# A fused short convolution and two-matrix SiLU block on one core: from 96-row chunks and PE transposes to two streams in 64-row halves of the array, in a pinned order

## The chip, the cores and the metric

The kernel runs on one core of a Trainium2 chip. The metric is the device time of one execution in microseconds (us), on an otherwise idle chip. Engines are named as the profile names them: PE is the matrix engine (PEld its weight loads), DVE the vector engine, ACT the activation engine, POOL and SP the two engines that here mostly issue DMAs. PSUM is the memory that PE writes its products to; "bank" stands here for one of the two parts, `[:, 0]` and `[:, 1]`, of a product tile in it; an eviction is the instruction that reads them out of it.

## The reference, cut to what matters

```python
# x: (8, 4096, 192)   weight: (8 heads, 7 taps)   w_in: (192, 2048)   w_out: (2048, 192)   beta: (2048,)
w   = softmax(weight, axis=-1)                      # one set of 7 taps for each group of 24 columns
c   = causal_conv7(x, w)                            # along the 4096 tokens; zeros before each batch's first token
h   = c.reshape(32768, 192) @ w_in
g   = h * sigmoid(beta * h)                         # = SiLU(beta * h) / beta
out = g @ w_out                                     # (32768, 192), float32
```

There are 32768 tokens. The first product contracts 192 columns, which does not split evenly into 128 rows, the most that a matmul in these traces has (L205 of the kernel before). The second contracts 2048.

## The kernel before

Tokens go through in 64 tiles of 512. Each tile is loaded (with a cast to bf16), transposed on PE, copied out of PSUM by DVE, convolved by DVE with columns on partitions, multiplied by `w_in` in two chunks of 96 rows, put through SiLU by ACT, and multiplied by `w_out`. `beta` is multiplied into `w_in` and divided out of `w_out` during start-up.

```python
for st in range(N_ST):                              # 64 tiles of 512 tokens
    nc.gpsimd.dma_start(out=x_bf, in_=x_view[st])
    ...                                             # L137/L138: 8 PE transposes into ptr, L142/L143: DVE copies
    for cw, xt, ct, rows in ((cw_a, xt_a, ct_a, DA), (cw_b, xt_b, ct_b, DB)):   # DA = DB = 96
        nc.vector.tensor_scalar_mul(ct[:rows, :], xt[:rows, 0:ST_TOK], cw[:rows, 0:1])
        for k in range(1, K - 1):
            nc.vector.scalar_tensor_tensor(out=ct[:rows, :], in0=xt[:rows, k:k + ST_TOK], ...)     # L163
        nc.vector.tensor_tensor(ct[:rows, :], xt[:rows, K - 1:K - 1 + ST_TOK], ct[:rows, :], ALU.add)  # L171
    for pair in range(NF // 2):                     # first product: NF = 16 chunks of 128 outputs
        ph = psum_h.tile([128, 2, ST_TOK], FP32)
        for i in range(2):
            fc = 2 * pair + i
            nc.tensor.matmul(ph[:, i, :], w_in_sa[:DA, ts(fc, 128)], ct_a[:DA, :], start=True, stop=False)  # L183
            nc.tensor.matmul(ph[:, i, :], w_in_sb[:DB, ts(fc, 128)], ct_b[:DB, :], start=False, stop=True)  # L190
        nc.scalar.activation(g_t[:, 2 * pair:2 * pair + 2, :], ph, AF.Silu)                        # L197
    for half in range(N_BLK // 2):                  # second product: 4 blocks of 128 tokens
        po = psum_o.tile([128, 2, D], FP32)
        for j in range(2):
            for fc in range(NF):
                nc.tensor.matmul(po[:, j, :], g_t[:, fc, ts(2 * half + j, BLK)], w_out_s[:, fc, :], ...)   # L205
        nc.vector.tensor_copy(o_sb[:, 2 * half:2 * half + 2, :], po)
    nc.sync.dma_start(out=out_view[st], in_=o_sb)
```

Nothing in it fixes the order in which an engine's work is issued; the framework's scheduler chooses it.

## Time and profile before

| | before |
|---|---|
| time, median of 4 runs | 1061.03 us |
| PE busy | 902.9 us, 85% |
| DVE, ACT busy | 60%, 48% |
| mean granted PE clock | 0.932 |
| PE waiting for the convolution | 114 us in 16 waits |

First the busy line of the page, its PE and PE-clock rows (40 equal slices, tenths), and three groups of instructions of the kernel before. A group's columns are: line, engine, operation, output and inputs, shapes, count | busy us, mean ns of one | idle time of the engine just before them, and what ended most of it.

```profile
PE 902.9 (85%) x6656; PEld 581.1 (55%) x6656; DVE 635.5 (60%) x1313; ACT 503.7 (48%) x516; POOL 49.1 (5%) x70
...
PE   1699798897979979799797988979799797997968
...
PEclk9999899898998989899898998989989899998989
...
L197 ACT ACTIVATE g_t<-ph 128x1024 bf16<-128x1024 f32 x512 | 500.5, 1021 | 540.8 <-PE ph L190 539.6
L183 PE MATMUL ph<-ct_a,w_in_sa 96*128 96x512 bf16 x1024 | 411.9, 402 | 118.7 <-DVE ct_a L171 114.3
...
L205 PE MATMUL po<-w_out_s,g_t 128*128 128x192 bf16 x4096 | 386.9, 247 | 2.7
```

The mean of 402 ns is the time from a matmul's start to its end, and matmuls overlap. What counts is the distance between starts. It is read in the timeline of PE (start us, length us, what; in brackets the idle time before and who ended it). Here is a stretch with a stall:

```profile
311.35 0.22 PE L138 MATMUL ptr<-ident,x_bf 128*96 128x128 bf16 x1
318.34 0.58 PE L183 MATMUL ph<-ct_a,w_in_sa 96*128 96x512 bf16 x1 [6.77 <-DVE ct_a L171]
318.73 0.63 PE L190 MATMUL ph<-ct_b,w_in_sb 96*128 96x512 bf16 x1
319.15 0.63 PE L183 MATMUL ph<-ct_a,w_in_sa 96*128 96x512 bf16 x1
...
325.25 0.38 PE L183 MATMUL ph<-ct_a,w_in_sa 96*128 96x512 bf16 x1
325.47 0.38 PE L190 MATMUL ph<-ct_b,w_in_sb 96*128 96x512 bf16 x1
```

The wait for the convolution over the whole run is one line of the list of waits (who waited for whom: us in total, times, longest):

```profile
PE ph L183 <- DVE ct_a L171: 114.3, 16, 11.4
```

In the stretch above, PE stands for 6.77 us until DVE has finished a convolution, then starts a 512-column matmul only every 0.425 us, and is back at 0.215 us some seven microseconds later. These are half and full clock: the view of windows gives a granted clock of 0.51 from 318.3 to 325.0 us and of 1.00 from 325.25 to 330.0 us. The clock record in the packed trace has the same after each of the 15 waits for the convolution that follow start-up (14 of 6.77 us, one of 8.12): a stretch at 0.50 that begins within the wait and lasts until 3.5 to 6.9 us after it.

### The profile page before, as it was taken

To read this page: it belongs to the slowest core of one execution; us is meant where nothing else is said; L and a number is where in the kernel's file an instruction comes from. 1 tells how busy PE (TensorE), PEld (TensorE's weight loads), DVE (VectorE), ACT (ScalarE), POOL (GpSimd) and SP (SyncE) were. 2 spreads that over 40 slices of the span, in tenths; PEclk is the share of its full clock that TensorE was granted. 3 is DMA by queue.
4 is the path that set the end of the run, shared out by engine and by line. 5 is a ranking of instruction groups with operands and counts; after the bars stand their busy time and mean duration, and the time that the engine had idled before them with its cause. 6 is when DMAs were issued, how large, how long until landed. Compare 5 with 4: busy or idle time off the path is not lost.

```text
span 1059.0 us, 15609 instructions
## 1 busy us (share of the span) xinstructions
PE 902.9 (85%) x6656; PEld 581.1 (55%) x6656; DVE 635.5 (60%) x1313; ACT 503.7 (48%) x516; POOL 49.1 (5%) x70
## 2 busy tenths in 40 slices
PE   1699798897979979799797988979799797997968
PEld 1366466464655646466464664646556464664645
DVE  5874564847547485464946548475474854649461
ACT  1355364453535535355353644535355352553534
POOL 2000000000000000000000000000000000000000
PEclk9999899898998989899898998989989899998989
DMA  9111312112130121301212121121201213012100
GB/s 208 12 38 38 53 32 42 32 38 38 38 54 15 38 39 38 53 16 38 41 45 44 32 43 31 38 38 38 53 16 38 38 38 53 16 38 39 37 16 31
DMA packets 72438, 42.96 MB, mean 41 GB/s; under 512 B 37232, under 2 KB 72048, under 8 KB 72048
## 3 DMA queue, kind: packets, MB, share of 16 engines
q0 software_dynamic: 33792, 12.59, 10.9%
q1 hardware_dynamic: 38576, 29.38, 8.7%
q8 instruction: 52, 0.85, 0.3%
q14 instruction: 18, 0.15, 0.0%
HBM read 29.37 MB, written 25.17 MB: 52 GB/s over the span
## 4 chain that ended last, share of the span: by engine, by line
PE 78%; DVE 13%; ACT 4%; DMA 2%; issue 1%; SPq 0%; ACTq 0%
PE po L205 33%; PE ph L183 24%; PE ph L190 21%; DVE ct_b L163 5%; DVE ct_a L163 5%; ACT g_t L197 4%; DMA beta_t<-in_moe_beta_dram 2%; DVE o_sb L212 1%; DVE ct_a L171 1%; DVE xt_b L143 1%; DVE xt_a L142 0%; DVE ct_b L159 0%; DVE ct_a L159 0%; DVE w_out_s L123 0%; SPq L78 0%
## 5 line engine op out<-in xcount | busy, mean ns | idle before, releaser
L197 ACT ACTIVATE g_t<-ph 128x1024 bf16<-128x1024 f32 x512 | 500.5, 1021 | 540.8 <-PE ph L190 539.6
L183 PE MATMUL ph<-ct_a,w_in_sa 96*128 96x512 bf16 x1024 | 411.9, 402 | 118.7 <-DVE ct_a L171 114.3
L190 PE MATMUL ph<-ct_b,w_in_sb 96*128 96x512 bf16 x1024 | 411.0, 402 | 0.0
L205 PE MATMUL po<-w_out_s,g_t 128*128 128x192 bf16 x4096 | 386.9, 247 | 2.7
L205 PEld LDWEIGHTS <-g_t 128*128 128x128 bf16 x4096 | 343.1, 98 | 71.0 <-ACT g_t L197 17.1
L212 DVE COPY o_sb<-po 128x384 f32<-128x384 f32 x128 | 71.1, 556 | 381.2 <-PE po L205 381.2
L163 DVE SCALAR_TENSOR_TENSOR ct_b<-xt_b,cw_b,ct_b 96x512 bf16<-96x512 bf16 x320 | 236.7, 740 | 0.0
L163 DVE SCALAR_TENSOR_TENSOR ct_a<-xt_a,cw_a,ct_a 96x512 bf16<-96x512 bf16 x320 | 236.6, 739 | 0.0
L190 PEld LDWEIGHTS <-w_in_sb 96*128 96x128 bf16 x1024 | 103.6, 101 | 233.2 <-issue 158.5
L183 PEld LDWEIGHTS <-w_in_sa 96*128 96x128 bf16 x1024 | 103.5, 101 | 125.8 <-issue 34.1
L133 POOL DMA_DIRECT2D x_bf<-in_x_dram x64 | 48.5, 760 | 905.1 <-PE ptr L138 903.9
L137 PE MATMUL ptr<-ident,x_bf 128*96 128x128 bf16 x256 | 39.1, 226 | 30.5 <-DMA x_bf<-in_x_dram 15.6
L137 PEld LDWEIGHTS <-x_bf 128*96 128x96 bf16 x256 | 31.0, 127 | 39.1 <-issue 17.5
L142 DVE COPY xt_a<-ptr 96x512 bf16<-96x512 bf16 x64 | 26.5, 413 | 22.4 <-PE ptr L138 22.4
L138 PE MATMUL ptr<-ident,x_bf 128*96 128x128 bf16 x256 | 38.6, 224 | 0.0
L138 PEld LDWEIGHTS <-x_bf 128*96 128x96 bf16 x256 | 31.0, 128 | 4.4
L171 DVE TENSOR_TENSOR ct_b<-xt_b,ct_b 96x512 bf16<-96x512 bf16 x64 | 26.5, 413 | 0.0
L171 DVE TENSOR_TENSOR ct_a<-xt_a,ct_a 96x512 bf16<-96x512 bf16 x64 | 26.4, 412 | 0.0
L143 DVE COPY xt_b<-ptr 96x512 bf16<-96x512 bf16 x64 | 26.2, 410 | 0.0
L159 DVE TENSOR_SCALAR ct_a<-xt_a,cw_a 96x512 bf16<-96x512 bf16 x64 | 23.0, 360 | 0.0
L159 DVE TENSOR_SCALAR ct_b<-xt_b,cw_b 96x512 bf16<-96x512 bf16 x64 | 21.8, 340 | 0.0
L150 DVE COPY xt_b<-xt_b 96x6 bf16<-96x6 bf16 x56 | 9.0, 160 | 0.0
(30 smaller groups left out, 25.8 us busy)
## 6 DMA issues: line engine op xcount, KB each, us to landing
out_dram<-o_sb SPq DMA_DIRECT2D x64, 384.0 KB
x_bf<-in_x_dram POOLq DMA_DIRECT2D x64, 192.0 KB, 5.2
w_out_t<-in_moe_w_out_dram SPq DMA_DIRECT2D x1, 1536.0 KB
beta_bc<-in_moe_beta_dram SPq DMA_DIRECT2D x1, 1024.0 KB
w_in_a<-in_moe_w_in_dram SPq DMA_DIRECT2D x1, 768.0 KB
w_in_b<-in_moe_w_in_dram SPq DMA_DIRECT2D x1, 768.0 KB
cw_a<-in_weight_dram SPq DMA_DIRECT2D x4, 0.7 KB
cw_b<-in_weight_dram SPq DMA_DIRECT2D x4, 0.7 KB
```

The lines of the kernel that those rows point to most:

```text
L133: nc.gpsimd.dma_start(out=x_bf, in_=x_view[st])
L137: nc.tensor.transpose(ptr[:DA, blk, :], x_bf[:, blk, 0:DA], ident)
L138: nc.tensor.transpose(ptr[:DB, N_BLK + blk, :], x_bf[:, blk, DA:D], ident)
L143: nc.vector.tensor_copy(xt_b[:DB, PAD:], ptr[:DB, N_BLK : 2 * N_BLK, :])
L159: nc.vector.tensor_scalar_mul(ct[:rows, :], xt[:rows, 0:ST_TOK], cw[:rows, 0:1])
L163: nc.vector.scalar_tensor_tensor(out=ct[:rows, :], in0=xt[:rows, k : k + ST_TOK], scalar=cw[:rows, k : k + 1], in1=ct[:rows, :], op0=mybir ...
L171: nc.vector.tensor_tensor(ct[:rows, :], xt[:rows, K - 1 : K - 1 + ST_TOK], ct[:rows, :], mybir.AluOpType.add,)
L183: nc.tensor.matmul(ph[:, i, :], w_in_sa[:DA, ts(fc, 128)], ct_a[:DA, :], start=True, stop=False,)
L190: nc.tensor.matmul(ph[:, i, :], w_in_sb[:DB, ts(fc, 128)], ct_b[:DB, :], start=False, stop=True,)
L197: nc.scalar.activation(g_t[:, 2 * pair : 2 * pair + 2, :], ph, AF.Silu)
L205: nc.tensor.matmul(po[:, j, :], g_t[:, fc, ts(blk, BLK)], w_out_s[:, fc, :], start=(fc == 0), stop=(fc == NF - 1),)
L212: nc.vector.tensor_copy(o_sb[:, 2 * half : 2 * half + 2, :], po)
```

## The change

The intent is to fill the array in the first product and to take everything else off PE.

- **Two streams in two halves.** The tokens are split into two streams of 16384. Columns of stream 0 live on partitions 0 to 63, those of stream 1 on 64 to 127; 192 columns are three chunks of 64. `w_in` is held on both halves. A matmul of stream 0 uses rows 0 to 63 of the array and one of stream 1 rows 64 to 127, so that the two can run together, if the array allows it.
- **The second product in halves too.** So that the array keeps one row tiling through the steady steps, each 128-row contraction is two 64-row ones, one in each half. The kernel keeps the halves from writing one PSUM bank at a time: they start on different banks and swap banks later ("phase").
- **A pinned order, one step ahead.** A unit is one `fc` of the first product of step i, a sixteenth of the second product of step i-1, and two DVE operations of the convolution of step i+1.
- **DMA transposes** in place of PE transposes, and **beta** as the activation's scale.
- **Start-up**: the first 128 tokens of each stream are convolved on PE by matmuls with shifted identities, and the first steps are short (128, 128, 256 tokens).

The core of the diff; start-up, launch and much of the bookkeeping are cut:

```diff
-        ptr = psum_tr.tile([128, 2 * N_BLK, BLK], BF16)
-        for blk in range(N_BLK):
-            nc.tensor.transpose(ptr[:DA, blk, :], x_bf[:, blk, 0:DA], ident)
-            nc.tensor.transpose(ptr[:DB, N_BLK + blk, :], x_bf[:, blk, DA:D], ident)
...
+            pin(nc.sync.dma_start_transpose(
+                out=xt_of[j][:, :, c:c + 128],
+                in_=xbf_of[j][:, b, :, :, :].rearrange("p k s c -> p (k s c)")))
...
+    def mm1(i, fc):
+        n = steps[i][1]
+        ph = psum_h.tile([128, NS, TILE], FP32, name="ph")
+        for kk in range(NK):                                     # NK = 3 chunks of 64
+            for s in range(NS):                                  # NS = 2 streams
+                r = slice(64 * s, 64 * s + 64)
+                pin(nc.tensor.matmul(ph[:, s, 0:n], w_in_s[r, kk, ts(fc, 128)], xc_of[i][r, kk, 0:n],
+                                     start=(kk == 0), stop=(kk == NK - 1)))
+        pin(nc.scalar.activation(g_of[i][:, fc, :, 0:n], ph[:, :, 0:n], AF.Silu,
+                                 scale=beta[:, fc:fc + 1]))
...
+    def mm2(i, pr, phase, fc):
...
+        for half in range(2):
+            q = half ^ phase                                     # bank of this half in this phase
+            s, b = pr[q]
+            r = slice(64 * half, 64 * half + 64)
+            pin(nc.tensor.matmul(po[:, q, 0:D], g_of[i][r, fc, s, ts(b, 128)], w_out_s[r, fc, :],
+                                 start=(phase == 0 and fc == 0), stop=(phase == 1 and fc == NF - 1)))
...
+        for u in range(NF):
+            mm1(i, u)
+            for t in plan[u]:                                    # 8 calls of mm2, in full steps
+                mm2(i - 1, *t)
+            for op in conv[:2]:                                  # convolution of step i + 1
+                op()
+            conv = conv[2:]
```

## The prediction

> **What bounds it now.** TensorE, by its own work and by a stall. In the PE timeline, a 512-column matmul follows the last every 0.215 us, a 192-column one every 86 ns (45 in 3.89 us), a transpose every 55 ns. Over 64 tiles: first product 2048 x 0.215 = 440 us, second 4096 x 0.0864 = 354 us, transposes 28 us: 822 of 1059 us. The rest:
> - 36 us of start-up: the first matmul waits for the convolution until 30.2 us;
> - 114 us idle waiting for the convolution (the list of waits: PE ph from DVE ct_a, 16 waits; one of 6.8 us at 311 us), part of it in start-up, and 30 us before transposes;
> - after each stall matmuls run at half rate (0.425 us apart at 318 to 325 us); mean granted clock 0.932, worth about 70 us.
>
> DVE is 60% busy, ACT 48%: the stall is order, not load.
>
> **What the change does.**
> 1. K=192 becomes three 64-row chunks instead of two of 96; two streams use the two row halves at once. Per 1024 tokens: 48 pairs instead of 64 matmuls, 48 x 0.216 = 10.4 us instead of 13.8. Saves 108 us in all, all critical, if a pair takes the time of one.
> 2. The second product has the same array work, in 256 half-height matmuls and loads per 1024 tokens instead of 128. Ideal 128 x 86 ns = 11.0 us. Four instructions per 86 ns is one per 21 ns; the tightest the trace shows is one per 28 ns (transposes). I estimate 86 to 105 ns a pair. [...] The bank handover has two units of other work between its phases, so I cost it at 0.
> 3. Transposes go to the DMA: 28 us off PE, their copies (53 us) off DVE. Four DMA transposes per step; x loads in smaller pieces triple the packets.
> 4. The conv is issued a step ahead, two ops per unit, in pinned order: the 114 us stall and most of the cold clock go.
> 5. DVE per 1024 tokens: 18 x 0.665 + 3 x 0.55 + 4 x 0.49 = 15.6 us. ACT: 16 x 0.97 = 15.5 us. Both under PE's 21.4 to 24, so PE still binds. Beta as activation scale costs nothing.
> 6. Start-up: first product at about 14 us instead of 30.
>
> **Sum.** 15 + 32 x (21.4 to 24.0) + 4 = 704 to 787. **Predicted 745 us, 8 in 10 within 695 to 825.** Faster by over 2%: 0.97; within 2%: 0.01; slower: 0.02.
>
> **What would show it.** Steps of 21 to 24 us; two matmuls of opposite halves starting within some ns, pairs 216 ns apart in the first product and 86 to 105 in the second; clock near 1.0; PE waits for DVE and ACT under 10 us after start-up; DVE about 500 us and ACT about 510 us busy; no PE transposes.
>
> **What would make it wrong.** Row tiles that do not overlap fully (each 10% of pair time is 70 us); weight loads of both halves serialising (110+ ns a pair in the second product); DMA transposes or small packets too slow, seen as DVE waits for DMA; the ph buffers making PE wait for ACT; a lower clock from denser work.

That two loads would hide under 86 ns, that two row halves would run at once, and that a change of tiling or a shared bank would cost anything was assumed; run 4 measures the change of tiling, no run the bank. The trace of the kernel before had only the lengths of the loads (98 ns for 128 columns, L205; 127 for 96, L137). The trace of the kernel after shows the rest: the matmuls of two halves start 19 ns apart, and in the second product a pair, with its two loads, follows the last every 82.5 ns. Point 5 has beta as scale for nothing; run 5 measured 90 ns an activation.

## More of the kernel before

A slot is the distance between the starts of two matmuls that follow each other.

## The result, and the profile after

| | before | after |
|---|---|---|
| time, median of 4 runs | 1061.03 us | 714.69 us (712.91 to 714.89) |
| ratio | | 0.6732, interval 0.6723 to 0.6742 |
| PE busy | 85% of 1059.0 us | 97% of 711.2 us |
| DVE, ACT busy | 635.5, 503.7 us | 502.2, 578.8 us |

A ratio is the mean time of one kernel's runs over that of the other's runs of the same rounds, so it is not quite the ratio of the medians quoted beside it.

The same parts of the page for the kernel after, with the shares of the chain of waits by engine (its fourth part):

```profile
PE 687.7 (97%) x11379; PEld 524.5 (74%) x11379; DVE 502.2 (71%) x877; ACT 578.8 (81%) x552; POOL 218.2 (31%) x290
...
PE   5589999999999999999999999999999999999998
...
PE 93%; POOL 2%; DMA 2%; DVE 2%; issue 0%; ACT 0%; SPq 0%; DVEq 0%; POOLq 0%
```

And the groups, from the list that keeps shapes apart:

```profile
L259 ACT ACTIVATE g<-ph,beta 128x1024 bf16<-128x1024 f32 x496 | 551.1, 1114 | 96.3 <-PE ph L257 92.3
L293 PE MATMUL po<-w_out_s,g 64*128 64x192 bf16 x7936 | 422.4, 243 | 0.0
L257 PE MATMUL ph<-xc,w_in_s 64*128 64x512 bf16 x2976 | 410.7, 376 | 3.1 <-DVE xc L231 3.1
```

PE waits for the convolution 3.1 us in the whole run, where it waited 114 us:

```profile
PE ph L257 <- DVE xc L231: 3.1, 3, 2.6
```

In the timeline of PE a steady unit reads so:

```profile
299.82 0.83 PE L257 MATMUL ph<-xc,w_in_s 64*128 64x512 bf16 x6
300.47 0.84 PE L293 MATMUL po<-w_out_s,g 64*128 64x192 bf16 x16
301.13 0.83 PE L257 MATMUL ph<-xc,w_in_s 64*128 64x512 bf16 x6
...
320.08 0.84 PE L293 MATMUL po<-w_out_s,g 64*128 64x192 bf16 x16
320.74 0.83 PE L257 MATMUL ph<-xc,w_in_s 64*128 64x512 bf16 x6
```

Six matmuls of 512 columns take 0.65 us from start to start of the next piece, that is 0.216 us for two. Sixteen of 192 columns take 0.66 us, 82.5 ns for two. The single starts, read from the packed trace record by record (the views merge neighbours), show the pairs (ns after 300 us; the first two rows are first product, the third second product):

```
 35   54        <- both halves, 19 ns apart
251  270
468  487  550  569  632  651  714  734 ...
```

A unit takes 1.307 us and a step of 16 units 20.92 us. Thirty-two times that is 669 us; the other 42 us are start-up and end. In the stretch of a full step PE has no idle time (columns: stretch, length, busy us and count of each engine, PE clock, DMA share, GB/s), while in the first full step it lacks 3 us:

```profile
48.80:69.70 20.90, 17.80 (x244) 11.65 (x244) 19.41 (x32) 17.07 (x19) 17.26 (x23) 1.00 1.07 92
300.00:320.90 20.90, 20.90 (x354) 16.01 (x352) 15.42 (x26) 17.81 (x17) 6.16 (x8) 1.00 0.52 78
```

So PE bounds the kernel after, at full rate (granted clock 1.00), with DVE at 74% and ACT at 85% of a step.

### The profile page after: what moved, and what is told of

Same layout as the page of the kernel before. It is cut to its first block, busy times and chain, and to the rows that moved or that the text cites. A ratio compares the mean times of both kernels' runs of the same rounds, so it can differ in the third digit from the quotient of the medians.

```text
span 711.2 us, 25346 instructions
## 1 busy us (share of the span) xinstructions
PE 687.7 (97%) x11379; PEld 524.5 (74%) x11379; DVE 502.2 (71%) x877; ACT 578.8 (81%) x552; POOL 218.2 (31%) x290
## 4 chain that ended last, share of the span: by engine, by line
PE 93%; POOL 2%; DMA 2%; DVE 2%; issue 0%; ACT 0%; SPq 0%; DVEq 0%; POOLq 0%
PE ph L257 46%; PE po L293 46%; PE po L316 2%; DVE acc L231 1%; POOL x_bf L96 1%; DMA w_in_s<-w_in_s 1%; DMA x_bf<-in_x_dram 1%; POOL w_in_s L80 0%; ACT g L259 0%; DVE xc L231 0%; DVE acc L229 0%; SPq L142 0%; POOL mask L132 0%; POOL mask L134 0%; DVE o_sb L320 0%
## 5 line engine op out<-in xcount | busy, mean ns | idle before, releaser
L259 ACT ACTIVATE g<-ph,beta 128x1024 bf16<-128x1024 f32 (+2 forms) x544 | 574.9, 1064 | 111.8 <-PE ph L257 107.4
L257 PE MATMUL ph<-xc,w_in_s 64*128 64x512 bf16 (+2 forms) x3264 | 432.7, 367 | 17.0 <-DMA w_in_s<-w_in_s 9.4
L293 PEld LDWEIGHTS <-g 64*128 64x128 bf16 x7936 | 359.6, 94 | 101.5
L293 PE MATMUL po<-w_out_s,g 64*128 64x192 bf16 x7936 | 422.4, 243 | 0.0
L231 DVE SCALAR_TENSOR_TENSOR acc<-xt,taps,acc 128x512 f32<-128x512 bf16 (+2 forms) x495 | 326.7, 727 | 0.0
L96 POOL DMA_DIRECT2D x_bf<-in_x_dram x256 | 197.5, 774 | 366.7 <-DMA xt<-x_bf 349.4
L257 PEld LDWEIGHTS <-w_in_s 64*128 64x128 bf16 x3264 | 168.2, 96 | 74.6 <-DMA w_in_s<-w_in_s 10.5
L231 DVE SCALAR_TENSOR_TENSOR xc<-xt,taps,acc 128x512 bf16<-128x512 bf16 (+2 forms) x99 | 66.5, 727 | 0.0
L229 DVE TENSOR_SCALAR acc<-xt,taps 128x512 f32<-128x512 bf16 (+2 forms) x99 | 41.8, 481 | 9.2 <-DMA xt<-x_bf 8.1
L207 POOL TENSOR_SCALAR w_out_s<-w_out_f,rbeta 128x192 bf16<-128x192 f32 x16 | 15.6, 992 | 0.1
```

The source lines that it names most:

```text
L96: pin(nc.gpsimd.dma_start(out=t[:, b, :, s, :], in_=src.rearrange("p (k c) -> p k c", c=64)))
L207: pin(nc.gpsimd.tensor_scalar_mul(w_out_s[:, c, :], w_out_f[:, c, :], rbeta[:, c:c + 1]))
L229: pin(nc.vector.tensor_scalar_mul(a, src, w))
L231: pin(nc.vector.scalar_tensor_tensor(out=xc[:, kk, 0:n] if k == K - 1 else a, in0=src, scalar=w, in1=a, op0=ALU.mult, op1=ALU.add))
L257: pin(nc.tensor.matmul(ph[:, s, 0:n], w_in_s[r, kk, ts(fc, 128)], xc_of[i][r, kk, 0:n], start=(kk == 0), stop=(kk == NK - 1)))
L259: pin(nc.scalar.activation(g_of[i][:, fc, :, 0:n], ph[:, :, 0:n], AF.Silu, scale=beta[:, fc:fc + 1]))
```

## The experiments

Twelve runs. Each is told against the kernel before of the same rounds; those medians lay between 1061.03 and 1061.85 us.

### 1. Order alone

Theory: 200 of the 346 us have nothing to do with halves of the array. The rival says that DVE cannot feed the old layout, so that order alone gains little. The edit keeps the 96-row chunks, the PE transposes and the DVE copies, and changes only the loop:

```diff
+    for st in range(N_ST):
+        ...
+        for u in range(8):
+            mm1(st, u)                                # 4 matmuls and one SiLU
+            if st:
+                mm2(st - 1, u)                        # 8 matmuls
+            for op in conv[2 * u : 2 * u + 2]:        # convolution of tile st + 1
+                op()
+            if st + 2 < N_ST:
+                if u < N_BLK:
+                    transpose_blk(st + 2, u)
+                elif u == 7:
+                    fill(st + 2)
```

> The kernel before with one thing changed: the main loop is issued in a pinned order, one step ahead (first product of tile st, second product of tile st-1, convolution of tile st+1, PE transposes of tile st+2 interleaved in eight units). 96-row chunks, 128-row array, PE transposes and DVE copies stay. Theory (the stall for the convolution and the half clock after it are a matter of order alone): only the tensor work remains, 2048 x 0.2155 + 4096 x 0.0825 + 512 x 0.0555 = 807 us, plus about 36 us of start-up and 6 us at the end: 845 to 860 us, PE waits for the convolution under 10 us after start-up, clock above 0.98. Rival (DVE cannot feed this layout, the row tiles give most of the gain): over 950 us, with PE still waiting for DVE.

Measured: correct, 860.46 us (859.67 to 861.25), ratio 0.8109; the median lies 0.5 us above the forecast range. The list of waits of this run has one wait of PE for the convolution left, the one in start-up:

```profile
PE ph L185 <- DVE ct_a L171: 32.7, 1, 32.7
```

Apart from that half microsecond the theory holds, and the rival falls: DVE did the same convolution (637.3 us busy) and was never late. Order alone is worth 201 us.

### 2. Order, and DMA transposes

The same kernel with the transposes moved to the DMA (two 96-column chunks padded to 128):

```diff
-        pin(nc.tensor.transpose(ptr[:DA, blk, :], xbf[st][:, blk, 0:DA], ident))
-        pin(nc.tensor.transpose(ptr[:DB, N_BLK + blk, :], xbf[st][:, blk, DA:D], ident))
+        pin(nc.sync.dma_start_transpose(out=xts[st][:, :, c : c + BLK],
+                                        in_=xbf[st][:, blk, :, :].rearrange("p h c -> p (h c)")))
```

> As the run with the pinned order, and the transposes moved to DMA transposes (two 96-column chunks padded to 128), no PE transposes and no copies of them on DVE. Theory: exactly the 28 us of PE transposes go: 818 to 832 us. Rival: the DMA transposes arrive late or the mode of transposes never cost PE time, so the time is within 10 us of the pinned order alone or longer, with DVE waiting for the DMA.

Measured: correct, 831.58 us (830.20 to 832.03), ratio 0.7834. It is 28.9 us less than the pinned order alone, which is what 512 transposes 55.5 ns apart took of PE (from the first product to the last matmul it is 28.0 us less; the rest is an earlier start). What remains to after is 831.6 - 714.8 = 117 us. The first product alone accounts for 2048 x 0.2155 - 1536 x 0.2155 = 110 us of it, if a pair takes a single slot. The rest is start-up and end: this run's span of 829.7 us has 50 us beyond its 64 tiles of 32 x 0.2155 + 64 x 0.0825 us, after has 42.

### 3. The halves in turn

Is it the neighbourhood in the queue that makes two halves run together? The edit swaps two loops, so that three lower-half matmuls are followed by three upper-half ones.

```diff
-        for kk in range(NK):
-            for s in range(NS):
+        for s in range(NS):
+            for kk in range(NK):
```

> The kernel after, with the first product of each unit issued as three matmuls of the lower row half and then three of the upper half, in place of alternating halves. Same instructions, same results. Theory (the gain of the row tiles is that neighbours in the queue of opposite halves run at the same time, starts stay in program order): five slots of 0.2155 us per unit in place of three, 2 x 0.2155 x 16 x 31 = 214 us more, 915 to 940 us. Rival (each half has its own stream, order inside a unit does not matter): 715 us.

Measured: correct, 715.78 us (715.24 to 716.42), ratio 0.6747. My theory falls. The unit looks as it does after, and the starts still come in pairs, now 26 ns apart:

```profile
300.84 0.83 PE L257 MATMUL ph<-xc,w_in_s 64*128 64x512 bf16 x6
301.49 0.84 PE L293 MATMUL po<-w_out_s,g 64*128 64x192 bf16 x16
302.15 0.83 PE L257 MATMUL ph<-xc,w_in_s 64*128 64x512 bf16 x6
```

The edit pins the order lower, lower, lower, upper, upper, upper. No kept view shows the order in the built program or the rows of a single matmul, so which is which is inferred: two 512-column matmuls of one half start 0.216 us apart (run 8), so two that start 26 ns apart are of different halves. So the upper half's first matmul overtook two of the lower half. In run 7 the same can be read from the lines of the kernel.

### 4. The second product over 128 rows

This takes away the odd part of the design, the second product in halves with its swap of banks. It leaves the same array time and half the instructions. The theory is that a change between 64-row and 128-row matmuls costs time; the rival, that it is free.

```diff
-        for half in range(2):
-            q = half ^ phase
-            s, b = pr[q]
-            r = slice(64 * half, 64 * half + 64)
-            pin(nc.tensor.matmul(po[:, q, 0:D], g_of[i][r, fc, s, ts(b, 128)], w_out_s[r, fc, :],
+        s, b = pr[phase]
+        pin(nc.tensor.matmul(po[:, phase, 0:D], g_of[i][:, fc, s, ts(b, 128)], w_out_s[:, fc, :],
```

> The kernel after, with the second product as full 128-row matmuls (half as many instructions, one bank after the other, no handover), the first product still in 64-row tiles. Array time of a unit is the same, 8 x 82.5 ns. Theory [...]: at the one such change that the trace of after has, at 697.41 us, the next matmul starts about 0.11 us later than the cadence; two per unit, 32 per step, 31 steps: 109 us more, about 820 us (780 to 880). Rival (changing is free, and the 64-row form of the second product buys nothing): 715 us within 1%.

Measured: correct, 822.80 us (821.38 to 824.95), ratio 0.7756, 108 us over after. A unit now takes 1.52 us:

```profile
301.13 0.82 PE L257 MATMUL ph<-xc,w_in_s 64*128 64x512 bf16 x6
301.88 0.83 PE L290 MATMUL po<-w_out_s,g 128*128 128x192 bf16 x8
302.65 0.82 PE L257 MATMUL ph<-xc,w_in_s 64*128 64x512 bf16 x6
```

In the single starts, the step from 64 to 128 rows comes 93 ns late and the matmul after it 10 ns; the step back is 96 and 11 ns late. That is 0.21 us a unit, and 0.21 x 16 x 31 = 104 us. The rival falls; why a change takes this time is not shown. Without halves in the second product, nearly all that the halves bring in the first (about 110 us) would be lost again.

### 5. Beta as a constant

```diff
-                                 scale=beta[:, fc:fc + 1]))
+                                 scale=1.0))
```

> The kernel after with the activation's scale as the constant 1.0 in place of the column beta; wrong result on purpose. One eviction of 128x1024 took 1021 ns before and 1114 ns after, so the forecast that beta as scale costs nothing was wrong by 93 ns. Theory: the column operand costs it; without it 1021 ns, ACT busy about 46 us less, and the time stays at 715 us within 0.5%, because ACT is not what PE waits for. Rival 1: the 93 ns come from the new layout of g or ph, so it stays at 1114 ns. Rival 2: ACT does hold PE back, and the time falls by over 1%.

Measured: wrong result, as intended; 714.25 us (714.06 to 714.55), ratio 0.6729. The eviction is back at its old length:

```profile
L259 ACT ACTIVATE g<-ph 128x1024 bf16<-128x1024 f32 x496 | 507.4, 1024 | 141.7 <-PE ph L257 141.6
```

The column operand costs 1114 - 1024 = 90 ns each. ACT's 44 us less do not move the time, which shows that ACT is not what PE waits for. Both rivals fall.

### 6. Both streams in one half

If the gain of the first product is that two halves work at once, it must vanish when all six matmuls use one half.

```diff
-                r = slice(64 * s, 64 * s + 64)
+                r = slice(0, 64)
```

> The kernel after, with all six matmuls of a unit's first product in the lower row half (both streams read the lower half's data; wrong result on purpose). Instructions, columns and loads are the same. Theory (the gain of the first product is that the two halves run at the same time): six slots of 0.2155 us in place of three, 3 x 0.2155 x 16 x 31 = 321 us more, 1020 to 1050 us. Rival (a 64-row matmul is by itself quicker than a 96-row one, or the second product hides it): under 900 us.

Measured: wrong result, as intended; 1982.95 us (1981.85 to 1983.44), ratio 1.868. This is far beyond the theory as well as the rival. The timeline of a unit, with single starts at 427 ns for 512 columns and 160 ns for 192:

```profile
302.63 1.91 PE L257 MATMUL ph<-xc,w_in_s 64*128 64x512 bf16 x4
303.92 0.34 PE L293 MATMUL po<-w_out_s,g 64*128 64x192 bf16 x1
304.34 0.63 PE L257 MATMUL ph<-xc,w_in_s 64*128 64x512 bf16 x1
```

The number of slots is as forecast (6 x 0.427 + 8 x 0.160 = 3.84 us a unit), but each is at half clock (427 ns where the kernel after has 216). The view of cores gives a clock of 1.000 for this run. That figure counts from the first change in the clock record, and the first release here is at 1969 us; from 60 to 1960 us the median distance of its 512-column matmuls is 427 ns. Another of the four runs, as long as this one (1981.85 us), is listed at 0.505.

### 7. Eleven in turn

How far may one half overtake the other? Each unit issues its eleven lower-half matmuls, then its eleven upper-half ones.

```diff
-            mm1(i, u)
-            for t in plan[u]:
-                mm2(i - 1, *t)
+            for half in range(2):
+                mm1(i, u, half)
+                for t in plan[u]:
+                    mm2(i - 1, *t, half)
```

> The kernel after, with each unit's eleven lower-half matmuls (three of the first product, eight of the second) issued first and then its eleven upper-half ones. The run with three in turn took 715.8 us against a forecast of 915 to 940: its six matmuls still started in pairs 26 ns apart, so halves start out of program order. Theory now (each half has a stream of its own and the queue reaches at least 22 instructions ahead): 712 to 725 us. Rival (the queue reaches only some ten instructions ahead): the halves run partly in turn, over 850 us, up to about 1350 with no overlap.

Measured: correct, 1051.49 us (1048.91 to 1052.01), ratio 0.9908: nearly all of the change's gain is gone. The rival holds. The timeline shows where the overlap starts:

```profile
300.11 0.57 PE L299 MATMUL po<-w_out_s,g 64*128 64x192 bf16 x5
300.45 0.39 PE L261 MATMUL ph<-xc,w_in_s 64*128 64x512 bf16 x1
300.52 0.33 PE L299 MATMUL po<-w_out_s,g 64*128 64x192 bf16 x2
300.68 0.38 PE L261 MATMUL ph<-xc,w_in_s 64*128 64x512 bf16 x1
300.69 0.24 PE L299 MATMUL po<-w_out_s,g 64*128 64x192 bf16 x1
300.89 0.38 PE L261 MATMUL ph<-xc,w_in_s 64*128 64x512 bf16 x1
```

Five of eight matmuls of one half have started when the first of the other half does (300.45); the remaining three are overtaken. So it started only when three of the matmuls issued before it were left. In the next run, too, just three are overtaken (at 301.26 us of its timeline). So a matmul of one half does start before ones of the other half that were issued earlier, three of them with their loads at most in the stretches read of these two runs. Whether matmuls, instructions or something else are counted, no run separates, and the rival's ten instructions are not shown either.

### 8. One half, with the clock released first

Was the half clock of run 6 caused by working in one half, or had the clock just never been released? The first six steps keep both halves.

```diff
-                r = slice(64 * s, 64 * s + 64)
+                r = slice(64 * s, 64 * s + 64) if i < 6 else slice(0, 64)
```

> The run with one half took 1983 us, not the forecast 1020 to 1050: its 512-column matmuls stood 427 ns apart and the 192-column ones 160 ns, half rate to the end, and the clock record shows the first release of the throttle only at 1969 us. Here the first six steps keep both halves as in the kernel after and only the other 28 use one half for the first product (wrong result on purpose). Theory (the half rate in that run was a clock that had never been released, the forecast of slots was right): released at about 34 us and kept, 28 x 16 units of 1.95 us in place of 1.307: 715 + 288 = 985 to 1020 us. Rival (one busy half is itself run at half rate): the clock falls back after step 6 and it takes over 1700 us.

Measured: wrong result, as intended; 1007.36 us (two runs, 1004.50 and 1010.21), ratio 0.9488. From 62.5 us to the last microseconds the clock stays at full rate (1.00 from 165 to 331 us and from 900 to 960 us in the view of windows), and a unit takes 1.955 us:

```profile
300.60 1.02 PE L257 MATMUL ph<-xc,w_in_s 64*128 64x512 bf16 x4
301.26 0.25 PE L293 MATMUL po<-w_out_s,g 64*128 64x192 bf16 x1
301.46 0.38 PE L257 MATMUL ph<-xc,w_in_s 64*128 64x512 bf16 x1
...
302.56 1.02 PE L257 MATMUL ph<-xc,w_in_s 64*128 64x512 bf16 x4
```

The estimate 714.8 + 28 x 16 x (1.955 - 1.307) gives 1005 us. So the slots were forecast rightly in run 6. The gain of the first product is that halves run at the same time, and a 64-row matmul is no quicker than a 96-row one (0.216 us from start to start here, 0.2155 before). Why run 6 was not released before 1969 us, while run 7 was and held (512-column matmuls 0.21 to 0.23 us apart from 300.45 to 300.89 us), stays open.

### 9 to 12. Start-up

Of the 42 us beyond the steady steps, 3 us follow the last matmul (708.1 to 711.2 us); the rest is lost before 70 us. I tried two other orders.

```diff
     load_w_in(1, 0, 512)
     ...
+    load_w_in(0, 512, 1024)
+    load_w_in(1, 1024, 1536)
+    load_w_in(0, 1536, 2048)
     load_x(0, 0, 4)
     ...
+            if i == 0 and u >= 4:          # 12 of 16 pieces of w_out scaled on ACT instead of POOL
+                pin(nc.scalar.activation(w_out_s[:, u - 4, :], w_out_f[:, u - 4, :], AF.Copy, scale=rbeta[:, u - 4:u - 3]))
```

> The kernel after with another start-up: all loads of the first weights are issued before the loads of x, the copies to the other half before the transposes and the loads of the second weights, and 12 of 16 pieces of the second weights are scaled on ACT during the first step in place of on POOL. Of the 42 us that after spends beyond 32 x 20.9 us, PE waits 9.4 us for copies of the first weights (at 15 to 29 us) and then for the convolution of the first full step, which ends at 53.7 us. Theory (start-up order is what is lost there, about 9 us of it): the convolution of the first full step ends at about 44 us, 703 to 711 us. Rival (the DMA engines, full in this stretch, set it): within 3 us of after.

Measured: correct, 712.63 us (712.54 to 712.74), ratio 0.6714. That is 2 us, not 9: the rival is nearer.

The second order moves the mask and two of the transposes up:

```diff
+    mask = ...                             # made before the loads of x are issued
     load_w_in(0, 512, 1024)
     ...
     for c in range(0, NF, 4):
         pin(nc.sync.dma_start(out=w_out_f[:, c:c + 4, :], in_=w_out_v[:, c:c + 4, :]))
-    transpose_x(0, 2, 4)
+        if c == 4:
+            transpose_x(0, 2, 4)
```

> The other start-up (712.6 us) once more: the mask of the taps is made before the loads of x are issued (DVE waited 5.5 us for it), and the transposes of the third and fourth block go ahead of half of the loads of the second weights (DVE waited 8 us for transposes). Theory (DVE's chain of three convolutions, which ends at 51.7 us there, sets the first full step): it starts some 5 us earlier and ends at about 47 us: 706 to 710 us. Rival (the DMA engines, over 100% busy from 10 to 30 us, set it, so what is moved up pushes something else back): 711 to 714 us.

Measured: correct, 717.96 us (716.74 to 718.71), ratio 0.6757: slower than after, and worse than the rival's range. The second weights now came late (POOL waited 9.7 us for them), PE's second product of a short step waited for POOL, and DVE stood 8.6 us before copying that product out. So the convolution of the first full step, which comes after this copy in the pinned order, ended at 57.2 us, not at 47:

```profile
43.10 0.56 DVE L299 COPY o_sb<-po 128x384 f32<-128x384 f32 x1 [8.63 <-PE po L291]
55.21 2.06 DVE L229 SCALAR_TENSOR_TENSOR xc<-xt,taps,acc 128x512 bf16<-128x512 bf16 x3
```

The clock may have added to it, which no run separates: its record in this run is at half rate again from 35.2 to 42.0 us and from 55.6 to 62.5 us, and that of after's profiled run is not. The stretch from 10 to 20 us in this run shows two more things: a DMA share above 1, which means that the times of packets overlap on the DMA engines, and a PE clock of 0.50.

```profile
10.00:20.00 10.00, 4.16 (x54) 2.55 (x51) 1.60 (x10) 2.77 (x8) 8.94 (x12) 0.50 1.86 190
```

To see whether the 2 us of the first order are real, it ran beside after on one chip.

> The kernel after, unchanged, beside the other start-up on the same chip, because the difference of the two (712.6 and 714.7 us, in different sessions) is 0.3%. If it is real: 714 to 715 us here.

> The first other start-up once more, beside after on the same chip. If its gain is real: 1.5 to 2.5 us under after, with no overlap of the runs. If not: within 1 us of after.

Measured: after 714.83 us (714.53 to 715.22), ratio 0.6738; the other start-up 711.59 us (710.76 to 712.13), ratio 0.6705, both correct. The runs do not overlap. The gain is 3.2 us, 0.45%, a little over the forecast of 1.5 to 2.5 us, and this is the fastest version here. That busy DMA engines set the rest of the start-up is argued from the share and from the two orders; no run takes the traffic away.

## Why the prediction was right, point by point

The forecast was 745 us within 695 to 825; the time was 714.69 us. It held because its mechanisms were right, and it came out 30 us high because two terms were off in opposite ways. That is partly luck: with start-up as short as forecast the time would have been about 692 us (an estimate, 714.7 - 23), just under the range.

| step of the forecast | forecast | measured |
|---|---|---|
| stall for the convolution and cold clock go, by order | 114 + 30 + 70 us | 201 us (run 1, whose own start-up is longer: first product at 41.6 us, not 30.2) |
| transposes leave PE | 28 us | 28.9 us (run 2) |
| first product, pairs in place of single matmuls | 108 us, pairs 216 ns apart | about 110 of the 117 us between run 2 and after; 216 ns |
| second product, ns a pair | 86 to 105 | 82.5 |
| a step of 1024 tokens | 21.4 to 24.0 us | 20.92 us |
| start-up and end | 15 + 4 us | 42 us |
| DVE, ACT busy | about 500, 510 us | 502.2, 578.8 us |
| beta as activation scale | nothing | 90 ns each, off the critical path (run 5) |
| handover of banks | nothing | nothing: a unit is 3 x 0.2155 + 8 x 0.0825 = 1.307 us |

- **The second product's term was too large twice.** The 86 ns came from dividing a piece of 3.89 us by its 45 matmuls. Such a piece ends with the last one's end, 0.247 us after its start, so the distance is (3.89 - 0.247) / 44 = 83 ns, and the second product before took 339 us and not 354. The surcharge up to 105 ns assumed that one instruction per 28 ns was near a limit. After, four instructions go through in 82.5 ns, one per 21 ns. Against the middle of the forecast the two are worth 32 x (22.7 - 20.92) = 57 us.
- **Start-up was too small.** The forecast counted the first matmul of the first product (about 14 us; measured 10.9) and took the kernel to be steady from there. It is not. PE waits 9.4 us for copies of weights (the list of waits names them), its matmuls run at half rate until about 34.5 us, and the convolution of the first full step ends only at 53.7 us. In all, start-up and end took 23 us more than forecast; how much each part has of it was not separated. The half rate can be read from starts: pairs of 128-column matmuls are 107 ns apart at 30 us and 55 ns at 37 us. In the timeline of the start eight warming matmuls on zeros are 0.42 us apart, though the clock column there says full:

```profile
1.25 3.60 PE L176 MATMUL ph<-zeros 128*128 128x512 bf16 x8 [1.25 <-DVE one L112]
```

- **ACT.** The forecast gave an activation with a column operand the length of one without. ACT had room: 17.8 of 20.9 us of a step.
- **The chances** (0.97 for faster by over 2%) were right; the feared limits, loads that serialise, late DMA transposes and a lower clock, did not appear in the steady part (82.5 ns a pair; from 300 to 320.9 us PE idle for 0 us and a granted clock of 1.00). In start-up DVE did wait 8.1 us for DMA transposes.

Of the 346 us, then, 201 come from order alone, 29 from the transposes, and 117 from the halves with the start-up. The halves, the most striking part of the change, are at most a third of its gain. The parts were added in this one sequence; halves without the pinned order were not run.

## What to carry to other kernels

When the costly engine waits for one that is only 60% busy, fix the order before the layout (201 of 346 us here): issue the slow engine's work one step ahead, in small pieces between the matmuls. In these runs, half-height matmuls of opposite row halves cost one slot for two (216 ns at 512 columns, 82.5 at 192) where they alternated or came three in turn (714.7 and 715.8 us) and the whole steady loop kept to one row tiling; eleven in turn took 1051.5 us, two changes of tiling a unit 822.8 us. Read a cadence from starts (82.5 ns here) and never from a merged piece's length over its count (86).
